# Two exp-value copies on ScalarE in the last two head pairs, and the early loads issued by SP

## The chip, the core and the metric

The program runs on one core of a Trainium2 chip. TensorE (PE) multiplies, VectorE (DVE), ScalarE (ACT) and GpSimd (POOL) work on what it leaves, and SyncE (SP) computes nothing and issues DMA transfers; ACT and POOL can issue transfers too, each on a queue of its own. The engines run side by side, each in the order of its own instructions, and wait for one another through semaphores. The metric is the device time of one execution in microseconds (us); less is better. Values are split in a high and a low part and multiplied in several passes to keep fp32 accuracy; much of the work beside PE's is copying out of the accumulation banks (PSUM) and splitting.

## The reference, cut to what matters

Causal attention with a decay bias over 2 x 8 heads, then two feed-forward layers on the 1152 tokens:

```python
scores = scale * q @ k.T + minimum(-(cum[:, None] - cum[None, :]), 0)   # causal, cum = cumsum(max(s, 0))
attn = exp(scores - max); attn = attn / (sum(attn) + 1e-9)
x = attn @ v                                    # 16 heads, S = 576, D = 64  ->  1152 x 512
x = x / sqrt(mean(x * x) + 1e-6) * rms_g
x = silu(x @ w_gate) * (x @ w_val) @ w_out      # 512 -> 1536 -> 512
h = x @ w_in                                    # 512 -> 2048
out = (h * tanh(log1p(exp(h)))) @ w_out2        # 2048 -> 512
```

## The kernel before, in words

The 16 heads are taken as 8 pairs (`NP = 8`), each in five units: units 0 to 3 are blocks of 128 query rows of one head (units 0 and 1 hold one block each's scores in one bank, 2 and 3 two banks), unit 4 is the last 64 rows of both heads. A unit goes through scores on PE (`qk_unit`), mask and row maximum on DVE (`maxes`, L468), exp on ACT (`exps`, L475), transposes of the exp values on PE (`pt_transposes`, L491), and their copies from PSUM to SBUF (`pt_evac`). For unit 3 these are two copies on DVE (L508, 128x384 and 128x512), for the other units they are on ACT (L510). After that come the products with V (`av_op`, L529, in two parts per pair), a copy to `XT` on ACT (`xt_evac`, L534), transposes back (L540) and the division by the row sums on DVE (`x_norm`, L559 and L563; the sums in `recips`, L546 to L549).

Three PSUM banks (`psT`) go round among the transposes of exp values, the transposes back and `xn_t` (L601). The last turns the normalized tokens of the first batch for the feed-forward layers while the last two pairs are computed; `xn_evac` takes it out, on ACT first (L607), and then on DVE (L608), which subtracts what ACT wrote.

Weights arrive as pieces of 512 KB (`w_load`, L315) and are unpacked by `wa` (ACT, L327), `wb` (DVE, L332 and L334) and `wc` (ACT L344, and POOL or DVE L346), one piece per pair during attention. For each pair there are loads of K and Q by POOL (L119, L122), of the cumulated sums (L125), of V (`load_v`, L140) and of the raw K and Q of the two heads (`load_raw`, L115), from which `k_lo` (L130) and `q_lo` (L136) make the low parts on POOL and DVE.

The order of every engine is written out by hand: the table `T` gives each operation a due position, counted in units (pair p begins at 5p), `at(position, function, ...)` collects all of them, and the list is run in order of the positions. An engine's instructions follow in that order, so moving a due position moves an operation in its engine's queue, and a transfer waits in the queue of the engine that issues it. In the kernel before, ACT issues `load_v` of pairs 1 to 3, `load_raw` of pairs 2 and 3, the first two weight pieces, and at the very start half of the raw of pair 0 (L151) and some constants; SP issues the rest.

Of the kernel before, what the change touches and what calls it, by code (L numbers as in the profile page):

```python
# [27 lines left out]
NP = B * H // 2  # L28
# [14 lines left out]
def tile_kernel(ctx: ExitStack, tc: tile.TileContext, kq, qq, v, s, w1, w2, rms_g, out):  # L43
    nc = tc.nc
# [449 lines left out]
    def pt_evac(i):  # L494
        p, u = divmod(i, 5)
        z, t = p % 2, t_tile.pop(i)
        if u < 2:
            cp = [(PTA[z][u], t[0][:, 0:384])]
        elif u < 4:
            cp = [(PTB[z][u - 2][:, 0:n, 128 * y:128 * y + 128], t[y][:, 0:128 * n].rearrange("p (c n) -> p c n", c=n))  # L500
                  for y, n in enumerate((3, 4))]
        else:
            cp = [(PTB[z][h][:, :, 256:320], t[0].rearrange("p (c n) -> p c n", c=4)[:, :, 64 * h:64 * h + 64])
                  for h in range(2)]
            cp += [(PTC[z][h], t[1][0:64, 64 * h:64 * h + 64]) for h in range(2)]
        for dst, src in cp:
            if u == 3:
                nc.vector.tensor_copy(out=dst, in_=src)  # L508
            else:
                nc.scalar.copy(out=dst, in_=src)  # L510
# [426 lines left out]
    def strassen(g, gaps):  # L937
# [33 lines left out]
    T = {  # L971
        "pt": (2.34, 2.02, 2.12, 2.44, 2.43), "exp": (1.65, 1.57, 0.62, 1.65, 0.84),
        "ev": (2.45, 2.48, 2.75, 2.63, 2.73), "max": (0.53, 0.2, 0.61, 0.6, 0.56), "av0": (4.48, 5.38),
        "av1": (7.66, 8.04, 8.29, 7.78, 8.36), "xte": (5.91, 9.16), "xtr": (7.48, 9.22), "rec": 6.44,
# [14 lines left out]
    def at(t, f, *args):  # L989
        events.append((t, len(events), f, args))  # L990
# [44 lines left out]
    for i in range(NU):  # L1035
        u, o = i % 5, pos[i]
        at(o, qk_unit, i)
        at(o + T["pt"][u], pt_transposes, i)
        at(o + T["exp"][u], exps, i)
        at(o + T["ev"][u], pt_evac, i)  # L1040
        at(o + T["max"][u], maxes, i)
    for p in range(NP):
        i = 5 * p
        z = "z" if p == NP - 1 else ""
        for x in range(2):
            for c, o in enumerate(T[f"av{x}{z}"]):
                at(i + o, av_op, p, x, c)
            at(i + T["xte" + z][x], xt_evac, p, x)
            at(i + T["xtr" + z][x], x_transposes, p, x)
            at(i + T["xn" + z][x], x_norm, p, x)  # L1050
        at(i + T["rec" + z], recips, p)
        if NP - NA <= p:
            n = p - NP + NA
            at(i + T["wa"], wa, n)
            if p + 1 < NP:
                at(i + T["wb"][0], wb, n, 0)
                at(i + T["wb"][1], wb, n, 1)
                at(i + T["wc"], wc, n)
        if p + 1 < NP:
            q1 = nc.scalar if p < 3 else nc.sync  # L1060
            if p:
                at(i + 0.3, load_raw, p + 1, q1)
                at(i + 0.2, load_k, p + 1)
                at(i + 0.2, load_q, p + 1)
            at(i + (T["lcum"] if p else -5.4), load_cum, p + 1)
            at(i + T["lv"], load_v, p + 1, q1)
            los, eng = (T["lo"], T["_le"]) if p else (T["lo0"], T["_l0"])
            for x in range(4):
                at(i + los[x], (k_lo, q_lo)[x % 2], p + 1, x // 2, nc.vector if eng[x] == "D" else nc.gpsimd)
    at(-7.02, load_v, 0, nc.sync)  # L1070
    at(T["lim1"], limit, 1, nc.scalar)
    at(T["lim8"], limit, 8, nc.scalar)
    for t in range(5):
        at(T["sq"][t], xn_sq, 0, t)
    for n in range(3):
# [184 lines left out]
```

## Time and profile before

| | us |
|---|---|
| median of three runs | 537.87 |
| runs | 535.26, 537.87, 539.09 |
| profiled execution | 534.09 |
| its span | 532.3 |

| engine | busy us | share of the span |
|---|---|---|
| PE | 522.0 | 98% |
| DVE | 376.3 | 71% |
| ACT | 278.4 | 52% |
| POOL | 58.7 | 11% |

The profile comes from one execution. Attention takes the first 112 us, the first feed-forward layer follows to about 336 us, and the second takes the rest. The mean granted TensorE clock is 0.986 of full speed. In the rows of a timeline the first two numbers are the start and the length in us; an engine's name with a q (ACTq, SPq) is its queue of transfers; in brackets stands how long the engine was idle before the operation and what ended that.

### The profile page before, as it was taken

To read this page: it belongs to the slowest core of one execution; us is meant where nothing else is said; L and a number is where in the kernel's file an instruction comes from. 1 tells how busy PE (TensorE), PEld (TensorE's weight loads), DVE (VectorE), ACT (ScalarE), POOL (GpSimd) and SP (SyncE) were. 2 spreads that over 40 slices of the span, in tenths; PEclk is the share of its full clock that TensorE was granted. 3 is DMA by queue.
4 is the path that set the end of the run, shared out by engine and by line. 5 is a ranking of instruction groups with operands and counts; after the bars stand their busy time and mean duration, and the time that the engine had idled before them with its cause. 6 is when DMAs were issued, how large, how long until landed. Compare 5 with 4: busy or idle time off the path is not lost.

```text
span 532.3 us, 7980 instructions
## 1 busy us (share of the span) xinstructions
PE 522.0 (98%) x2948; PEld 471.5 (89%) x2948; DVE 376.3 (71%) x787; ACT 278.4 (52%) x604; POOL 58.7 (11%) x72
## 2 busy tenths in 40 slices
PE   7999999999999999999999999999999999999997
PEld 4767777688999999999999999999889999999885
DVE  6799999954988777686578777487678667653321
ACT  5688997876353435354357655564424433333211
POOL 6245666310000000000000000000000000000000
PEclk8699999999999999999999999999999999999999
DMA  9989887212003243435155635254201000000101
GB/s 223 267 209 263 210 244 176 81 50 109 7 35 118 89 153 124 148 122 153 46 159 159 169 108 159 80 158 126 73 0 51 10 2 0 1 0 1 59 1 59
DMA packets 18782, 55.90 MB, mean 105 GB/s; under 512 B 2348, under 2 KB 2604, under 8 KB 18716
## 3 DMA queue, kind: packets, MB, share of 16 engines
q1 hardware_dynamic: 13520, 42.04, 25.6%
q0 software_dynamic: 3712, 9.70, 9.0%
q10 hardware_dynamic: 1512, 3.66, 2.3%
q8 instruction: 23, 0.38, 0.3%
q14 instruction: 15, 0.12, 0.1%
HBM read 52.73 MB, written 2.66 MB: 104 GB/s over the span
## 4 chain that ended last, share of the span: by engine, by line
PE 90%; DVE 5%; ACT 2%; DMA 2%; issue 1%; ACTq 0%; DVEq 0%
PE o L864 12%; PE gv L649 11%; PE y L794 9%; PE gv L818 8%; PE gv L667 6%; PE gv L864 6%; PE xa L529 5%; PE gv L794 5%; PE pc L691 5%; PE pd L691 5%; PE pa L691 4%; PE tp L491 4%; PE sc L443 2%; PE pb L691 2%; PE sc L444 2%; DMA r<-in_w_dram 1%
## 5 line engine op out<-in xcount | busy, mean ns | idle before, releaser
L649 PE MATMUL gv<-xh,wring 128*128 128x384 f32 x256 | 67.0, 338 | 0.2 <-DVE h_w L658 0.2
L327 ACT ACTIVATE r<-r 128x512 f32<-128x512 f32 x57 | 38.5, 679 | 31.3 <-DMA r<-in_w_dram 30.6
L334 DVE SCALAR_TENSOR_TENSOR r<-r 128x512 int32<-128x512 int32 x68 | 48.4, 712 | 3.3
L794 PE MATMUL y<-hhl,w 128*128 128x384 f32 x288 | 50.2, 334 | 0.0
L794 PEld LDWEIGHTS y<-hhl,w 128*128 128x128 f32 x288 | 49.9, 188 | 0.0
L649 PEld LDWEIGHTS gv<-xh,wring 128*128 128x128 f32 x256 | 46.4, 188 | 0.4 <-DVE h_w L658 0.3
L475 ACT ACTIVATE px<-sc,cst 128x384 f32<-128x384 f32 (+2 forms) x80 | 41.3, 530 | 6.3 <-DVE cst L468 6.3
L649 PE MATMUL gv<-xl,wring 128*128 128x384 f32 x128 | 43.0, 336 | 0.0
L667 PE MATMUL gv<-xh,wring 128*128 128x384 f32 x160 | 41.6, 336 | 0.0
L468 DVE CUSTOM_DVE_ANT_0 sc<-sc,xtm 128x384 f32<-128x384 f32 (+4 forms) x72 | 34.6, 500 | 4.8 <-PE sc L444 3.0
L491 PE MATMUL tp<-cst,px 128*128 128x128 f32 (+1 forms) x200 | 30.9, 285 | 1.9 <-DVE w L563 0.8
L685 DVE TENSOR_TENSOR glb<-u,glb 128x768 fp32r<-128x768 f32 x20 | 19.1, 955 | 15.9 <-ACT glb L684 15.7
L491 PEld LDWEIGHTS tp<-cst,px 128*128 128x128 f32 (+1 forms) x200 | 24.1, 144 | 6.7 <-issue 1.2
L529 PE MATMUL xa<-aw,px 128*64 128x320 f32 (+3 forms) x192 | 30.0, 380 | 0.0
L332 DVE TENSOR_SCALAR r<-r 128x512 int32<-128x512 int32 x68 | 29.3, 430 | 0.0
L667 PEld LDWEIGHTS gv<-xh,wring 128*128 128x128 f32 x160 | 29.0, 188 | 0.0
L864 PE MATMUL o<-wt,glb 128*128 128x512 f32 x108 | 26.9, 390 | 0.0
L667 PE MATMUL gv<-xl,wring 128*128 128x384 f32 x80 | 26.9, 336 | 0.0
L864 PE MATMUL o<-w,glb 128*128 128x512 f32 x108 | 26.5, 390 | 0.0
L346 DVE TENSOR_TENSOR w<-r,w 128x512 fp32r<-128x512 f32 x24 | 16.5, 688 | 13.8 <-ACT w L344 13.7
L776 ACT CAST hhl<-h_w 128x384 fp32r<-128x384 f32 x30 | 15.5, 516 | 19.3 <-PE y L794 12.8
L794 PE MATMUL gv<-hhl,w 128*128 128x384 f32 x144 | 25.1, 334 | 0.0
(268 smaller groups left out, 1258.0 us busy)
## 6 DMA issues: line engine op xcount, KB each, us to landing
r<-in_w_dram SPq DMA_DIRECT2D x66, 512.0 KB, 3.5
w<-in_kq_dram POOLq DMA_DIRECT2D x7, 576.0 KB, 6.2
w<-in_qq_dram POOLq DMA_DIRECT2D x7, 576.0 KB, 7.1
out_dram<-osb SPq DMA_DIRECT2D x8, 256.0 KB, 2.1
px<-in_v_dram SPq DMA_DIRECT2D x5, 320.0 KB
r<-in_w_dram ACTq DMA_DIRECT2D x2, 512.0 KB, 4.4
px<-in_v_dram ACTq DMA_DIRECT2D x3, 320.0 KB
raw_hA<-in_kq_dram SPq DMA_DIRECT2D x3, 288.0 KB
```

The lines of the kernel that those rows point to most:

```text
L327: nc.scalar.activation(out=top, in_=top, func=ACTF.Prelu, scale=2.0 ** -112, alpha=-2.0 ** 32)
L334: nc.vector.scalar_tensor_tensor(out=low, in0=top, scalar=3, in1=low, op0=ALU.logical_shift_left, op1=ALU.bitwise_or)
L468: nc.vector.tensor_tensor_reduce(out=sv, in0=sv, in1=m, scale=-0.125, scalar=first, op0=ALU.add, op1=ALU.min, accum_out=sbias[:, c:c + 1])
L475: nc.scalar.activation(out=pv, in_=sv, func=ACTF.Exp, bias=sbias[:, c + x:c + x + 1], scale=-1.0, accum_out=ssum[:, sc:sc + 1])
L491: nc.tensor.transpose(t[0:rows, o - a:o - a + 128], P[pos[i] % 2][:, o:min(e, o + 128)], ident)
L529: nc.tensor.matmul(o, V[z][0:rows, c, ds], r, start=(c == 0), stop=(c == (1, 4)[part]))
L649: nc.tensor.matmul(t[:, g, 0:TB], w[:, a, 128 * c:128 * c + 128], xhl[r][:, c, TB * b:TB * b + TB], start=(n == 0), stop=(n == 11))
L667: nc.tensor.matmul(t[:, g, 0:TB], w[:, a, 128 * c:128 * c + 128], xhl[r][:, c, TB * b:TB * b + TB], start=(n == 0), stop=(n == 11))
L691: nc.tensor.matmul(t, A[a][:, 128 * c:128 * c + 128], B[r][:, c], start=(start and n == 0), stop=(n == 5), skip_group_check=True)
L794: nc.tensor.matmul(y_t[b][d], w[:, a, 128 * d:128 * d + 128], hhl[:, r], start=(f == FY[0] and y == 0), stop=(f == FY[-1] and y == 2))
L818: nc.tensor.matmul(t[:, x, 0:TB], w[:, a, 128 * c:128 * c + 128], xhl[r][:, c, TB * b:TB * b + TB], start=(n == 0), stop=(n == 11))
L864: nc.tensor.matmul(o_t[b][tt], gl[:, r, x, 128 * tt:128 * tt + 128], w[:, a], start=(g == 0 and x == 0 and y == 0), stop=(g == NG - 1 and ...
```

## The change

In the last two pairs (p = 6 and 7) the two copies of unit 3 go to ACT. The weight operation `wa` of pair 7 is due 0.64 positions later and `wc` of pair 6's due list 0.35 later; in ACT's order that puts both behind `xn_evac` of the fourth quarter (due 40.73), `wc` first (40.80), then `wa` (40.85). All nine loads that ACT issued inside the loop over pairs are issued by SP (L151 and the constants stay), in their old order but for the second weight piece, which is due just behind `load_v` instead of just ahead of it.

```diff
         for dst, src in cp:
-            if u == 3:
+            if u == 3 and p < NP - 2:
                 nc.vector.tensor_copy(out=dst, in_=src)
             else:
                 nc.scalar.copy(out=dst, in_=src)
...
-        "lcum": 1.47, "lv": 3.58, "lim1": 2.19, "lim8": 8.49, "sq": (24.04, 23.82, 29.07, 27.0, 28.42),
+        "lcum": 1.47, "lv": 3.58, "lim1": 2.19, "sq": (24.04, 23.82, 29.07, 27.0, 28.42),
...
             n = p - NP + NA
-            at(i + T["wa"], wa, n)
+            at(i + T["wa"] + (0.64 if p == NP - 1 else 0), wa, n)
             if p + 1 < NP:
                 at(i + T["wb"][0], wb, n, 0)
                 at(i + T["wb"][1], wb, n, 1)
-                at(i + T["wc"], wc, n)
+                at(i + T["wc"] + (0.35 if p == NP - 2 else 0), wc, n)
         if p + 1 < NP:
-            q1 = nc.scalar if p < 3 else nc.sync
             if p:
-                at(i + 0.3, load_raw, p + 1, q1)
+                at(i + 0.3, load_raw, p + 1)
                 at(i + 0.2, load_k, p + 1)
                 at(i + 0.2, load_q, p + 1)
             at(i + (T["lcum"] if p else -5.4), load_cum, p + 1)
-            at(i + T["lv"], load_v, p + 1, q1)
+            at(i + T["lv"], load_v, p + 1)
...
-    at(T["lim1"], limit, 1, nc.scalar)
-    at(T["lim8"], limit, 8, nc.scalar)
+    at(T["lim1"], limit, 1)
+    at(T["lv"] + 5.01, limit, 8)
```

## Rows read from the trace of the kernel before

**Rows 1.** The page, busy tenths in 40 slices of the span, PE
```profile
PE   7999999999999999999999999999999999999997
```

**Rows 2.** Table of stages: length, then PE, PEld, DVE, ACT, POOL busy, clock, DMA
```profile
22.00:23.00 1.00, 1.00 (x5) 0.92 (x4) 0.00 (x0) 1.00 (x6) 0.01 (x1) 0.54 1.29 332
...
91.20:102.30 11.10, 9.73 (x69) 6.78 (x69) 10.63 (x33) 8.40 (x28) 5.20 (x7) 1.00 0.30 97
102.30:112.00 9.70, 8.96 (x68) 6.37 (x68) 7.07 (x21) 8.01 (x23) 1.54 (x2) 1.00 0.01 2
```

**Rows 3.** Timeline of PE, last two pairs
```profile
95.84 0.72 PE L491 MATMUL tp<-cst,px 128*128 128x128 f32 x5
...
108.96 0.30 PE L491 MATMUL tp<-cst,px 128*64 128x128 f32 x1 [0.47 <-DVE xl L608]
109.19 2.45 PE L529 MATMUL xa<-aw,px 128*64 128x320 f32 x20
```

**Rows 4.** Timeline of ACT, last two pairs
```profile
94.57 1.13 ACT L607 ACTIVATE xh<-bank,cst 128x512 fp32r<-128x512 f32 x2
...
104.42 0.98 ACT L510 COPY aw<-tp 128x384 f32<-128x384 f32 x2
...
106.30 0.68 ACT L327 ACTIVATE r<-r 128x512 f32<-128x512 f32 x1
...
107.43 0.89 ACT L607 ACTIVATE xh<-bank,cst 128x512 fp32r<-128x512 f32 x2
...
108.52 1.09 ACT L510 COPY aw<-tp 128x256 f32<-128x256 f32 x4
```

**Rows 5.** Timeline of DVE, last two pairs
```profile
94.40 1.15 DVE L508 COPY aw<-tp 128x384 f32<-128x384 f32 x2
95.47 0.94 DVE L608 SCALAR_TENSOR_TENSOR xl<-bank,cst,xh 128x512 fp32r<-128x512 f32 x2
...
108.15 0.94 DVE L608 SCALAR_TENSOR_TENSOR xl<-bank,cst,xh 128x512 fp32r<-128x512 f32 x2 [0.44 <-ACT xh L607]
```

**Rows 6.** Timeline of ACT and its queue, first two pairs
```profile
17.30 0.36 ACTq L140 DMA_DIRECT2D px<-in_v_dram  x1
17.50 0.37 ACT L475 ACTIVATE px<-sc,cst 128x128 f32<-128x128 f32 x1
...
29.25 0.33 ACTq L315 DMA_DIRECT2D r<-in_w_dram  x1
30.74 0.34 ACTq L140 DMA_DIRECT2D px<-in_v_dram  x1
31.12 0.43 ACT L534 COPY xtm<-xa 128x320 f32<-128x320 f32 x1 [1.40 <-PE xa L529]
...
34.41 0.45 ACTq L115 DMA_DIRECT2D raw_r<-in_kq_dram  x1
...
34.94 0.66 ACT L327 ACTIVATE r<-r 128x512 f32<-128x512 f32 x1
```

**Rows 7.** Timeline of DVE, pairs 1 and 2
```profile
28.84 1.89 DVE L334 SCALAR_TENSOR_TENSOR r<-r 128x512 int32<-128x512 int32 x1
...
40.70 0.69 DVE L334 SCALAR_TENSOR_TENSOR r<-r 128x512 int32<-128x512 int32 x1
```

**Rows 8.** Timeline of POOL, pairs 1 and 2
```profile
28.77 1.41 POOL L136 TENSOR_TENSOR w<-raw_hA,w 64x576 fp32r<-64x576 f32 x1 [6.76 <-DMA raw_hA<-in_kq_dram]
...
40.99 1.66 POOL L136 TENSOR_TENSOR w<-raw_mm,w 64x576 fp32r<-64x576 f32 x1 [2.89 <-DMA raw_mm<-in_kq_dram]
```

**Rows 9.** Timeline of PE, pairs 0 and 1
```profile
18.47 0.61 PE L450 MATMUL sc<-w 68*128 68x288 f32 x1 [0.42 <-ACT px L475]
...
35.51 0.74 PE L491 MATMUL tp<-cst,px 128*128 128x128 f32 x5 [0.84 <-DVE w L563]
```

**Rows 10.** View of one line, L315, the weight loads: time from issue to landing
```profile
DMA to landing us min/median/max: 3.4/3.6/5.3
```

**Rows 11.** DMA queues from 35 to 39 us: packets, MB, share
```profile
q10 hardware_dynamic: 8, 0.02, 1.5%
```

## The prediction

> **What bounds the kernel now.** I read the page's slices first: TensorE is 9 tenths busy or more in every slice but the first and the last [rows 1]. Time can be won or lost only where it stands still or where its clock is low, and what is lost ahead of such a stretch reaches the end unshortened. Then the stages: the edits touch two. Late, in the last two pairs, TensorE is busy 9.73 of 11.10 us and 8.96 of 9.70 us; the standing of 1.37 + 0.74 = 2.11 us is all that the late edits could ever win. [...]
>
> Then I read the timelines of the engines in the last two pairs. TensorE's rows show five transposes at 95.84 (unit 4 of pair 6) and, at 108.96, the last transpose of pair 7, held for VectorE's L608, directly ahead of the last 20 attention products at 109.19 [rows 3]. ScalarE is the fuller engine from 104.42 on: its rows follow one another without a hole up to the four copies at 108.52 [rows 4]. VectorE does the copies in question of pair 6 at 94.40 and then L608 at once [rows 5].
>
> **The late edits, step by step.** VectorE loses four copies, two in each pair; those of pair 6 take 1.15 us [rows 5]. ScalarE gains them. Their price there is seen in the same two shapes of unit 2: the two that begin at 104.42 take 0.98 us [rows 4]. What lies behind them in ScalarE's order decides.
>
> Pair 6: the copies come ahead of `xn_evac` (L607), which first starts at 94.57 [rows 4]. With 0.98 us before it that becomes about 95.5. VectorE's L608 needs L607's first half. In pair 7 L607 starts at 107.43 [rows 4] and L608, held by it, at 108.15 [rows 5], 0.72 us later. So L608 starts at 95.5 + 0.6 to 0.7 = 96.1 or 96.2, where it starts at 95.47 now [rows 5]: VectorE is given 1.15 us and waits them away. The fifth transpose of the row at 95.84 [rows 3] writes the bank that this L608 empties (three banks go round in the order in which the code asks for them). It comes about 0.5 us later, and with it all that TensorE has behind it. I take **+0.5**. Bounds: 0, if the bank is free earlier than I read; +0.98, the full copies.
>
> Pair 7: the two offsets put `wa` and `wc`, which run from 106.30 to 107.43 now, behind `xn_evac` [rows 4]. That clears 1.13 us for 0.98 us of copies, so L607 and L608 keep their places, and so does the transpose at 108.96. But `wa` and `wc` still stand ahead of the copies at 108.52 [rows 4], and those come 0.98 us later. The products at 109.19 [rows 3] read what they write. Four copies take 1.09 us [rows 4], so the two that the first products need end near 109.06; 0.13 us is spare and some 0.8 us shows. I take **+0.8**. Bounds: 0, if ScalarE gets there earlier; +0.98. VectorE's relief in pair 7 buys nothing: TensorE waits for it only through L608, which L607 times.
>
> Late edits together: 0.5 + 0.8 = **+1.3 us**, bounds 0 and +1.96.
>
> **The early edits, step by step.** ScalarE loses nine DMA issues. The one at 17.30 lasts 0.36 us, yet the exp behind it already starts at 17.50, so it is hidden; the one at 30.74 holds its successor 0.38 us, to 31.12, after 1.40 us in which ScalarE waited for the products anyway [rows 6]. VectorE is the late engine in that pair (below), so I count 0.
>
> SP issues in the order of the code. So the weight load of 29.25 stands behind load_v, which waits for the products until 30.74; it is issued at about 31.12, with 320 KB ahead of it. It must land before L327 at 34.94, which stands in ScalarE's order ahead of the exps [rows 6]. Loads of this kind land after 3.4 to 5.3 us [rows 10]: at 34.5 to 36.4, a stall of 0 to 1.5 us. I take 0, since the median of 3.6 gives 34.7. The upper end is what a tail caught by POOL's loads would bring: from 35 to 39 us the queue of ScalarE's loads moved 0.02 MB [rows 11], though raw loads had been issued on it up to 34.41 [rows 6].
>
> [...]
>
> The raw loads of pair 2 come forward, because SP does not stand behind exps. Today POOL's `q_lo` waits 6.76 us for them and starts at 28.77 [rows 8]. VectorE's L334, which starts at 28.84, then takes 1.89 us, where the same operation takes 0.69 a pair later [rows 7], and TensorE stands 0.84 us at 35.51 for VectorE [rows 9]. With raw early, POOL starts earlier, when its other input has landed. Bounds: -0.84, the whole stand won, if POOL is through before VectorE comes; +0.84, if two POOL operations block VectorE where one does now. I take **+0.3**: POOL then meets L332 as well as L334.
>
> **Sum.** 1.3 + 0.3 = +1.6 us. The profiled execution took 534.09 us (a span of 532.3 and 1.8 around it), which gives 535.7. It was faster than all the runs shown, 3.8 us under their median of 537.87, so against the median I predict **539.5 us**, 0.3% more.
>
> **Rivals.**
>
> [...] From pair 2 on the order is kept by a hair: VectorE's L334 starts at 40.70 [rows 7], POOL's `q_lo` at 40.99 [rows 8], 0.29 us later. POOL's start follows transfers, and a delay of TensorE moves those only a pair later. If pair 1 loses more than 0.29 us, or raw lands that much earlier, POOL is first, L334 waits, and the next pair starts late in turn. Price: 0.84 us of standing [rows 9] in each of five pairs, 4.2 us: 539.5 + 4.2 = 543.7 us, with a stalled L327 up to 545. Against it: pair 1 collides today and pair 2 recovers.
> [...]
>
> *B, the late cost is hidden.* ScalarE or the banks have more room than I read, both late steps cost nothing, and the move to SP only changes a queue: 537.87 + 0.3 = 538.2 us, no change.
>
> [...]
>
> **How the numbers follow.** Forecast 0.50, A 0.20, B 0.17, C 0.13. About 1% (5.4 us) is what a measurement of this kernel can tell from no change; the runs of before lie between 535.26 and 539.09. Slower by over 1%, above 543.2, takes A in full: 0.15. Faster by over 1%, under 532.5, needs C, the stand at 35.51 and a free late part at once: 0.04. Within 1%: 0.81. The range: below, C's 537.1 less 1.6 us for the spread of the runs, 535.5; above, A's 543.7, so 544. The forecast's own range is 537.5 to 541.5.
>
> **What would show it.** Late: L608 of pair 6 held by L607 with VectorE idle before it; the fifth transpose of unit 4 waiting for L608; the four copies of pair 7 starting after `wa`, and the 20 products behind them 1.3 us later, counted from the first products of pair 6. It is wrong if those 20 products come as early as now. Early: POOL's `q_lo` of pair 2 before 28.77, L332 or L334 long beside it, and TensorE standing at about 35.5 for 0.8 to 1.7 us. [...] If the total comes out right with none of these, the reasons were wrong.

## The result and the profile after

| kernel | runs | median us | lowest to highest | profiled execution | its span |
|---|---|---|---|---|---|
| before | 13 | 536.36 | 533.37 to 540.56 | 534.09 | 532.3 |
| after | 13 | 539.01 | 537.01 to 542.36 | 542.36 | 540.4 |

After takes 1.0061 of the time of before, 95% interval 1.0038 to 1.0084: 0.6% slower. The interval leaves out 1, so a difference under the 1% that the prediction took as its bound can be told from none. In this document a run over 1.5% above the quickest of its kernel counts as slow and is left out of ratios and medians, which takes one run from best_sp (544.60 us) and four from the runs of before beside fence, fence_after and both_late. The two profiled executions lie 8.27 us apart and the medians 2.65: the profile of after is the slowest of its thirteen runs, that of before a quick one. So I take positions inside a stage from the profiles, not their difference in total.

A simple measure of the late part is the distance from the seven transposes of unit 3 in pair 6 (L491) to the first gate product (L649), with those of pair 7 between them. First before, then after:

```profile
92.12 0.98 PE L491 MATMUL tp<-cst,px 128*128 128x128 f32 x7
...
105.97 0.98 PE L491 MATMUL tp<-cst,px 128*128 128x128 f32 x7
...
107.86 0.63 PE L491 MATMUL tp<-cst,px 128*128 128x128 f32 x4 [0.26 <-DVE aw L508]
...
111.76 0.42 PE L649 MATMUL gv<-xh,wring 128*128 128x384 f32 x1
```

```profile
99.44 0.98 PE L491 MATMUL tp<-cst,px 128*128 128x128 f32 x7
...
113.54 0.98 PE L491 MATMUL tp<-cst,px 128*128 128x128 f32 x7
...
120.45 0.42 PE L649 MATMUL gv<-xh,wring 128*128 128x384 f32 x1
```

In before it runs from 92.12 to 111.76 us, 19.64 us; in after from 99.44 to 120.45, 21.01 us. Up to pair 6, after is 7.32 us behind; in the late part it loses 1.37 more. Of the 7.32 us, 5.9 are there by 64 us, behind the two early stands shown below and a fallen clock after each (0.50 from 25 to 27 us and from 49 to 55). The rest comes behind 86 us, where TensorE stands 0.97 us for L608 at 96.92, in unit 2 of pair 6; late_only, with the loads of before, has the same stand (0.98 us), so it isn't put to the loads.

TensorE in the slices of the page of after (before: [rows 1]), and its granted clock under them:

```profile
PE   6898999889999999999999999999999999999997
...
PEclk9797999999999999999999999999999999999999
```

What is lost lies in the first nine slices, as in the prediction; the rest of the row is unchanged. The clock is down (7 tenths) in the second and the fourth slice and not in the last pairs.

The late part of after on TensorE, ScalarE and VectorE (start and length in us; answers to [rows 3 to 5]):

```profile
100.86 0.63 PE L601 MATMUL bank<-cst,w 128*128 128x128 f32 x4 [0.44 <-DVE w L563]
...
103.84 0.30 PE L491 MATMUL tp<-cst,px 128*64 128x128 f32 x1 [0.42 <-DVE xl L608]
...
116.58 0.30 PE L491 MATMUL tp<-cst,px 128*64 128x128 f32 x1 [0.72 <-DVE xl L608]
117.63 2.69 PE L529 MATMUL xa<-aw,px 128*64 128x320 f32 x20 [0.76 <-ACT aw L510]
```

```profile
101.44 0.97 ACT L510 COPY aw<-tp 128x384 f32<-128x384 f32 x2
102.28 0.92 ACT L607 ACTIVATE xh<-bank,cst 128x512 fp32r<-128x512 f32 x2
...
114.14 1.00 ACT L510 COPY aw<-tp 128x384 f32<-128x384 f32 x2
115.04 0.90 ACT L607 ACTIVATE xh<-bank,cst 128x512 fp32r<-128x512 f32 x2
115.82 0.66 ACT L344 CAST wring<-r 128x512 fp32r<-128x512 f32 x1
116.36 0.68 ACT L327 ACTIVATE r<-r 128x512 f32<-128x512 f32 x1
116.93 0.37 ACT L534 COPY xtm<-xa 128x256 f32<-128x256 f32 x1
117.18 0.85 ACT L510 COPY aw<-tp 128x256 f32<-128x256 f32 x4
```

```profile
103.03 0.94 DVE L608 SCALAR_TENSOR_TENSOR xl<-bank,cst,xh 128x512 fp32r<-128x512 f32 x2 [1.53 <-ACT xh L607]
...
115.77 0.94 DVE L608 SCALAR_TENSOR_TENSOR xl<-bank,cst,xh 128x512 fp32r<-128x512 f32 x2 [1.88 <-ACT xh L607]
```

In pair 6, ScalarE does its two copies and only then L607; VectorE, which has been given their time, stands 1.53 us for L607, and TensorE's fifth transpose 0.42 us for L608. In pair 7, L344 and L327 stand between L607 and the four copies, and the 20 products wait 0.76 us for those.

The early part of after, on DMA queues and engines, in order of the fences: SP's and GpSimd's issues, TensorE, VectorE, ScalarE.

```profile
15.13 0.33 SPq L315 DMA_DIRECT2D r<-in_w_dram  x1
15.51 0.43 SPq L140 DMA_DIRECT2D px<-in_v_dram  x1
15.98 0.43 SPq L115 DMA_DIRECT2D raw_hA<-in_kq_dram  x1
16.52 0.36 SPq L115 DMA_DIRECT2D raw_hB<-in_kq_dram  x1
```

```profile
16.25 0.56 POOL L125 DMA_DIRECT2D w<-scr  x1 [4.38 <-DMA cst<-in_rms_g_dram]
```

```profile
22.59 0.30 PE L444 MATMUL sc<-w 68*128 68x128 f32 x1 [1.41 <-DMA w<-scr]
...
48.34 0.45 PE L443 MATMUL sc<-w 128*128 128x128 f32 x1 [1.80 <-POOL w L130]
```

```profile
28.80 1.13 DVE L332 TENSOR_SCALAR r<-r 128x512 int32<-128x512 int32 x1
...
30.03 1.72 DVE L334 SCALAR_TENSOR_TENSOR r<-r 128x512 int32<-128x512 int32 x1
```

```profile
36.41 0.68 ACT L327 ACTIVATE r<-r 128x512 f32<-128x512 f32 x1 [0.34 <-DMA r<-in_w_dram]
```

The raw loads of pair 2 are issued before 17 us, where ScalarE issued them at 21.84 and 22.27. GpSimd is early in pair 1 and collides with L332 and L334, as forecast: its `q_lo` runs from 28.23 us for 1.40 and its `k_lo` from 29.71 for 1.49, and L332 takes 1.13 us beside the first and L334 1.72 beside the second, where the shortest of each in after take 0.42 and 0.69. But TensorE stands in two places that the prediction doesn't name, 1.41 us for the cumulated sums (`w<-scr`) and 1.80 us for `k_lo`. The second stand has a late transfer behind it too: GpSimd's load of Q for pair 3, issued at 34.75, takes 10.1 us to land, and `q_lo`, with `k_lo` behind it, starts at 44.98. In before the same load, issued at 33.17, takes 7.0 us, and `q_lo` starts at 40.99 [rows 8].

The table of stages of after, microsecond by microsecond (length, then PE, PEld, DVE, ACT, POOL busy, granted clock, DMA, GB/s; before: [rows 2]):

```profile
17.00:18.00 1.00, 0.99 (x5) 0.76 (x4) 0.97 (x3) 0.79 (x4) 1.00 (x1) 0.66 0.90 359
...
21.00:22.00 1.00, 0.18 (x1) 0.04 (x1) 0.60 (x3) 0.64 (x3) 0.56 (x2) 1.00 1.04 198
22.00:23.00 1.00, 0.41 (x3) 0.41 (x3) 0.00 (x0) 1.00 (x5) 0.00 (x0) 1.00 1.38 175
...
25.00:26.00 1.00, 1.00 (x7) 0.96 (x5) 0.72 (x4) 0.23 (x2) 0.00 (x0) 0.50 1.41 240
```

The clock leaves 0.50 in the microsecond from 17 and is at 1.00 before the stand, where before still has 0.54 at 22. Behind the stand it is at 0.50 again by 25 us. Both executions begin unit 3 of pair 0 at 23.47 us: the early rise is given back. The fall then costs 1.6 us more: the eight products (L529) that begin at 26.77 us in before begin at 28.35 in after.

### The profile page after: what moved, and what is told of

It reads as the page before. It is cut to its first block, busy times and chain, and to the rows that moved or that the text cites. A ratio compares the mean times of both kernels' runs of the same rounds, so it can differ in the third digit from the quotient of the medians.

```text
span 540.4 us, 7976 instructions
## 1 busy us (share of the span) xinstructions
PE 524.1 (97%) x2948; PEld 473.6 (88%) x2948; DVE 379.7 (70%) x783; ACT 280.6 (52%) x608; POOL 57.5 (11%) x72
## 4 chain that ended last, share of the span: by engine, by line
PE 87%; DVE 5%; ACT 3%; DMA 2%; issue 2%; SPq 1%; DVEq 0%; ACTq 0%
PE o L864 12%; PE gv L649 12%; PE y L794 9%; PE gv L818 8%; PE gv L667 8%; PE gv L864 6%; PE pa L691 5%; PE pc L691 5%; PE pd L691 5%; PE gv L794 5%; PE xa L529 4%; PE tp L491 3%; PE pb L691 2%; PE sc L443 2%; DVE sc L468 2%
## 5 line engine op out<-in xcount | busy, mean ns | idle before, releaser
L649 PE MATMUL gv<-xh,wring 128*128 128x384 f32 x256 | 67.1, 338 | 0.2 <-DVE h_w L658 0.2
L327 ACT ACTIVATE r<-r 128x512 f32<-128x512 f32 x57 | 38.4, 677 | 29.2 <-DMA r<-in_w_dram 29.0
L334 DVE SCALAR_TENSOR_TENSOR r<-r 128x512 int32<-128x512 int32 x68 | 50.3, 739 | 3.4
L649 PEld LDWEIGHTS gv<-xh,wring 128*128 128x128 f32 x256 | 46.4, 188 | 0.4 <-DVE h_w L658 0.3
L649 PE MATMUL gv<-xl,wring 128*128 128x384 f32 x128 | 43.0, 336 | 0.0
L491 PE MATMUL tp<-cst,px 128*128 128x128 f32 (+1 forms) x200 | 33.2, 298 | 2.8 <-DVE xl L608 2.1
L491 PEld LDWEIGHTS tp<-cst,px 128*128 128x128 f32 (+1 forms) x200 | 25.8, 152 | 8.4 <-DVE xl L608 2.8
L529 PE MATMUL xa<-aw,px 128*64 128x320 f32 (+3 forms) x192 | 30.1, 379 | 0.8 <-ACT aw L510 0.8
L332 DVE TENSOR_SCALAR r<-r 128x512 int32<-128x512 int32 x68 | 30.5, 448 | 0.0
L685 DVE TENSOR_TENSOR glb<-u,glb 128x768 fp32r<-128x768 f32 x20 | 19.1, 955 | 15.9 <-ACT glb L684 15.7
L443 PE MATMUL sc<-w 128*128 128x384 f32 (+1 forms) x64 | 25.5, 408 | 2.5 <-POOL w L130 1.8
```

What stands on the lines that cost most here:

```text
L327: nc.scalar.activation(out=top, in_=top, func=ACTF.Prelu, scale=2.0 ** -112, alpha=-2.0 ** 32)
L334: nc.vector.scalar_tensor_tensor(out=low, in0=top, scalar=3, in1=low, op0=ALU.logical_shift_left, op1=ALU.bitwise_or)
L491: nc.tensor.transpose(t[0:rows, o - a:o - a + 128], P[pos[i] % 2][:, o:min(e, o + 128)], ident)
L529: nc.tensor.matmul(o, V[z][0:rows, c, ds], r, start=(c == 0), stop=(c == (1, 4)[part]))
L649: nc.tensor.matmul(t[:, g, 0:TB], w[:, a, 128 * c:128 * c + 128], xhl[r][:, c, TB * b:TB * b + TB], start=(n == 0), stop=(n == 11))
```

## The experiments

All runs in one table. Pair 6 is the distance from unit 3's transposes in pair 6 to those in pair 7, pair 7 the one from there to the first gate product, both in the profiled execution. Ratios are to runs of the kernel before on the same chip; a single run has none.

| kernel | median us (runs) | ratio, 95% interval | pair 6 | pair 7 |
|---|---|---|---|---|
| before (profile) | 536.36 (13) | | 13.85 | 5.79 |
| after | 539.01 (13) | 1.0061 [1.0038, 1.0084] | 14.10 | 6.91 |
| late_only | 538.88 (12) | 1.0064 [1.0029, 1.0099] | 14.11 | 6.91 |
| loads_only | 537.52 (12) | 1.0023 [0.9994, 1.0052] | 13.85 | 5.79 |
| pair6_only | 537.82 (1) | | 15.67 | 5.79 |
| pair7_only | 536.63 (1) | | 13.49 | 6.92 |
| fence | 536.36 (12) | 0.9988 [0.9954, 1.0022] | 15.89 | 5.79 |
| fence_after | 539.86 (12) | 1.0095 [1.0066, 1.0125] | 15.90 | 8.53 |
| both_late | 535.50 (12) | 0.9986 [0.9953, 1.0018] | 13.87 | 5.81 |
| norm_first | 535.15 (12) | 0.9970 [0.9939, 1.0002] | 13.44 | 5.78 |
| best | 534.15 (12) | 0.9948 [0.9919, 0.9976] | 13.56 | 5.82 |
| best_sp | 536.82 (11) | 1.0005 [0.9974, 1.0037] | 13.93 | 5.81 |
| best_raw | 535.19 (12) | 0.9983 [0.9953, 1.0013] | 13.55 | 5.81 |
| best_noraw | 535.82 (12) | 1.0001 [0.9969, 1.0033] | 13.55 | 5.81 |

**The change in parts.** The late edits alone and the loads alone; then each pair's late edits alone.

```diff
-            if u == 3:
+            if u == 3 and p != NP - 2:      # pair6_only; pair7_only: p != NP - 1, with the two offsets of wa and wc
```

> The late edits alone (four copies on ScalarE, the two offsets), loads issued as before. Theory 1, both parts cost: about 1.4 us over before (ratio 1.002 to 1.003), and from the row of seven transposes of pair 6 to the first gate product 21.0 us, as in the changed kernel, against 19.64 before. Theory 2, the early loads cost everything and the longer last pairs follow from them: ratio 1.000 and 19.6 us. Theory 3, the late edits cost everything: ratio 1.005 to 1.006.

> All nine loads issued by SP, the late edits left out. Theory 1: about 1.3 us over before (ratio 1.002 to 1.003), the last pairs at 19.6 us, and the loss ahead of them, where TensorE waits for operands of K and Q that land late. Theory 2: ratio 1.005 to 1.006. Theory 3: ratio 1.000.

> Only the two copies of pair 6 on ScalarE, no offset. By the steps of the prediction TensorE loses 0.3 to 0.5 us between the seven transposes of pair 6 and those of pair 7 (13.85 us before, 14.10 in the changed kernel), because VectorE's L608 waits for L607. Rival: the loss there comes with the early loads, and this interval stays at 13.85.

> Only the two copies of pair 7 on ScalarE, with the two offsets. By the steps of the prediction the 20 products start 0.8 us later after the seven transposes of pair 7, and the first gate product comes 0.8 to 1.1 us later (5.79 us before, 6.91 in the changed kernel), since wa and wc stand ahead of the last copies. Rival: ScalarE catches up and it stays at 5.8.

The late edits give the late part of after to 0.01 us: 14.11 + 6.91 = 21.02. The loads alone leave it as it was, 19.64. In time the late edits are slower clear of noise, 3.4 us (0.0064 x 535.79), interval 1.6 to 5.3, which is nearer to theory 3 than to theory 1. The loads alone measure 1.2 us, interval -0.3 to 2.8, which fits both. On top of the late edits they show no cost: after, with both, has 1.0061, late_only 1.0064. TensorE does wait for operands of K and Q in loads_only, as theory 1 has it: 0.57 us for `k_lo` at 45.63, behind a load of Q that takes 9.4 us.

Pair 6 of pair7_only has the code of before and takes 13.49, not 13.85. TensorE's stands in pair 6, first the kernel before, then pair7_only:

```profile
93.90 0.63 PE L601 MATMUL bank<-cst,w 128*128 128x128 f32 x4 [0.80 <-DVE w L563]
```

```profile
95.53 0.63 PE L601 MATMUL bank<-cst,w 128*128 128x128 f32 x4 [0.44 <-DVE w L563]
```

The execution of before stood 0.36 us longer for L563, which is the whole 13.85 - 13.49. After and late_only stand 0.44 and 0.43 us there. So against its like the edit of pair 6 costs 14.10 - 13.49 = 0.61 us, and that of pair 7 6.91 - 5.79 = 1.12 us: 1.73 us together. Counted from unit 3's transposes, L608 of pair 6 starts 0.60 us later in after (3.59) than in pair7_only (2.99).

pair6_only was the surprise, 15.67 us for a pair that takes 14.11 in late_only. Tables of stages, three equal stretches from the start of unit 3's transposes, pair6_only and then late_only (which has the same code in this pair):

```profile
94.30:97.30 3.00, 2.00 (x16) 1.47 (x14) 2.03 (x7) 3.00 (x9) 0.79 (x1) 1.00 0.01 3
97.30:100.30 3.00, 2.57 (x13) 2.14 (x14) 2.31 (x8) 2.57 (x11) 3.00 (x5) 0.75 0.49 124
100.30:103.30 3.00, 3.00 (x16) 1.87 (x15) 2.87 (x10) 2.02 (x8) 0.22 (x1) 0.68 0.74 231
```

```profile
100.20:103.20 3.00, 1.99 (x17) 1.44 (x14) 2.07 (x7) 2.99 (x9) 0.75 (x1) 1.00 0.01 3
103.20:106.20 3.00, 2.58 (x18) 2.10 (x18) 2.28 (x8) 2.65 (x13) 3.00 (x5) 1.00 0.44 98
106.20:109.20 3.00, 3.00 (x21) 1.87 (x21) 2.87 (x10) 2.78 (x10) 0.26 (x1) 1.00 0.65 255
```

TensorE is busy to within 0.01 us alike, and in one execution the clock falls behind the stands and in the other it does not. That is 15.67 - 14.11 = 1.56 us.

**Is it GpSimd's collisions that make executions differ?** In the kernel fence GpSimd reads one element that L334 has written before it goes on, so that it never runs ahead of L332 and L334; fence_after is the changed kernel with the same.

```diff
-        "lo": (3.28, 3.14, 4.19, 4.89),
+        "lo": (3.48, 3.47, 4.19, 4.89),
...
+    def behind_wb(n):
+        nc.gpsimd.tensor_copy(out=fence_t, in_=conv[n][0:1, 0:1, 0])
...
+            if p:
+                at(i + 3.465, behind_wb, p - 1 - NP + NA)
```

> The kernel before, and in pairs 1 to 6 GpSimd reads one element of what VectorE's L334 wrote before it starts q_lo and k_lo of the next pair (their due positions go from 3.14 and 3.28 to 3.47 and 3.48), so that GpSimd is never ahead of L332 and L334. Theory 1, rival A of the prediction is what makes one execution differ from the next: wherever GpSimd is first, L332 or L334 takes 1.1 to 1.9 us, TensorE stands for VectorE, and the same code reaches pair 6 at 92.1 us in one execution and at 100.3 us in another. Then L332 and L334 take no more than 0.5 and 0.8 us in all pairs up to 105 us, pair 6's transposes of unit 3 start at 91 to 92.5 us, the median falls by 1 to 2.5 us against the kernel before (ratio 0.995 to 0.998) and the runs lie closer together, within 4 us. Theory 2, the executions differ by the time at which transfers land: the ratio is 1.000 within 0.002 and the runs lie over 6 us as before.

> The changed kernel with the same order between L334 and GpSimd. Theory 1: from unit 3 of pair 6 to the first gate product it takes 21.0 us (before 19.6), and its median lies above that of the fenced kernel before by the late edits alone, 1.2 to 1.6 us. Rival, the loads on SP cost something beside collisions (raw, V and weights of SP beside K, Q and the cumulated sums of GpSimd): above it by 2.5 us or more, with TensorE held for w<-scr near 22 us or for k_lo and q_lo that start late because K or Q landed late.

The view of L334 up to 105 us in fence (its shortest, median and longest duration in ns):

```profile
L334 DVE SCALAR_TENSOR_TENSOR r<-r x7: 693/695/699, 29.2 to 103.5; 128x512 int32<-128x512 int32 x7
```

The collisions are gone, and the runs still lie from 534.13 to 539.78 us with a ratio of 0.9988; pair 6's transposes of unit 3 start at 94.04 us, not at 91 to 92.5. Theory 1 falls: an L334 of 1.7 us or more is seen in before (1.89), after (1.72), pair6_only (1.71) and both_late (1.70), but collisions are not what makes executions differ. The ratio is the one that theory 2 gives, but nothing here tests its cause. What the rows show of a collision is its length: 1.89 us for the L334 that starts 0.07 us behind GpSimd's `q_lo` [rows 7, 8], against 0.70 at most here. What in the chip holds L334 they do not show.

fence_after lies 3.5 us above fence (539.86 - 536.36), and the signs of its rival are there: TensorE stands 1.69 us for `w<-scr` at 22.73 and 0.70 us for `k_lo` at 47.77. But late_only alone measured 3.4 us, so this difference can't be put to the loads.

The last pair of fence_after shows a fallen clock once more. TensorE's timeline there:

```profile
114.03 0.30 PE L491 MATMUL tp<-cst,px 128*64 128x128 f32 x1 [0.72 <-DVE xl L608]
115.08 4.33 PE L529 MATMUL xa<-aw,px 128*64 128x320 f32 x20 [0.75 <-ACT aw L510]
```

The two stands are those of after, but the 20 products take 4.33 us, not 2.69, under a lower clock (0.50 in the microseconds from 116 to 119; in after 1.00 throughout): pair 7 takes 8.53 us, 1.62 more, and the late part 24.4 us, not the 21.0 of theory 1. In pair 6, fence and fence_after take 15.9 us, with a fallen clock (0.50 from 98.04 to 101.04 us in fence, from 99.10 to 102.10 in fence_after) after two stands, of 1.25 or 1.26 and of 0.57 or 0.58 us.

**The order on ScalarE.** The copies stay on ScalarE in both pairs, and all weight work is put behind the copies of unit 4.

```diff
-            if u == 3:
+            if u == 3 and p < NP - 2:
...
-            at(i + T["wa"], wa, n)
+            at(i + T["wa"] + (1.64 if p >= NP - 2 else 0), wa, n)
...
-                at(i + T["wc"], wc, n)
+                at(i + T["wc"] + (1.35 if p >= NP - 3 else 0), wc, n)
```

> The kernel before; the two copies of unit 3 are on ScalarE in the last two pairs as in the change, but wa and wc are put behind the four copies of unit 4 in both pairs (wa 1.64, wc 1.35 positions later), not ahead of them. All loads as before. Theory, the steps of the prediction: what costs time is what stands ahead of L607 in pair 6 and ahead of the four copies in pair 7. With 1.2 us of weight work out of both places for 0.98 us of copies, pair 6 takes 13.5 to 13.9 us from unit 3's transposes to those of pair 7 (before 13.85, changed 14.10) and pair 7 takes 5.5 to 5.9 us from there to the first gate product (before 5.79, changed 6.91). Rival, ScalarE has simply too much work in the last two pairs and the order changes only where it shows: the sum from pair 6 to the gate product stays above 20.5 us. The time is that of the kernel before, ratio 0.998 to 1.002, by the theory, and 1.002 to 1.006 by the rival.

The last pair of both_late, ScalarE and then TensorE:

```profile
110.22 1.02 ACT L510 COPY aw<-tp 128x384 f32<-128x384 f32 x2 [0.16 <-PE tp L491]
111.14 0.90 ACT L607 ACTIVATE xh<-bank,cst 128x512 fp32r<-128x512 f32 x2
111.91 0.38 ACT L534 COPY xtm<-xa 128x256 f32<-128x256 f32 x1
112.17 0.68 ACT L510 COPY aw<-tp 128x256 f32<-128x256 f32 x2
```

```profile
112.67 0.30 PE L491 MATMUL tp<-cst,px 128*64 128x128 f32 x1 [0.72 <-DVE xl L608]
112.90 2.42 PE L529 MATMUL xa<-aw,px 128*64 128x320 f32 x20
```

The copies follow L607 with only L534 between them, and the products have no stand of their own. Pair 7 is back to 5.81 us, the sum to 19.68, with the same work on ScalarE. So in pair 7 the order costs the time, not the load, and the rival falls there. In pair 6 the order wins back part: 13.87 us, where the edit as made takes 14.10 and pair7_only, with the copies on VectorE, 13.49. The time, 0.9986 of before, can't be told from 1, and its interval (up to 1.0018) lies below that of late_only (from 1.0029): the order shows in the time too.

**A version that is faster.** norm_first puts VectorE's `q_lo` behind the division; best is both_late with that, and with the copies of pair 7 shared between VectorE and ScalarE.

```diff
-        "lo": (3.28, 3.14, 4.19, 4.89),
+        "lo": (3.28, 3.14, 4.19, 5.495),
...
+            if u == 3 and (p < NP - 2 or p == NP - 1 and y == 0):    # best: copy y = 0 of pair 7 stays on VectorE
```

> The kernel before, with VectorE's q_lo (L136) of every pair placed behind the division L559 and L563 instead of just ahead of it (due 5.495 instead of 4.89). In the looks so far TensorE stood for L563 once or twice in most executions: 0.84 us in the kernel before at 35.5 us, 1.79 with the late edits alone, 2.20 with the weight work behind, and 0.80 to 1.26 us ahead of L601 in pair 6. L136 takes 0.75 us. Theory 1, these stands are what VectorE's lateness costs, and the clock that falls behind one in some executions (from 1.00 to 0.50 for some 3.3 us, 1.6 to 2.0 us lost) is why executions differ: then the stands for L563 shrink by up to 0.75 us each, pair 6 takes 13.0 to 13.5 us instead of 13.85, and the median falls by 0.5 to 2 us (ratio 0.996 to 0.999). Theory 2, VectorE has the same work and is late one operation further on: the stands move behind L136 (TensorE waits for the scores of the next pair's second unit) and the ratio is 1.000 within 0.002.

> The weight work behind the unit-4 copies in both last pairs, L136 behind L563, and in pair 7 one of the two copies of unit 3 on VectorE and one on ScalarE; loads as before. Theory 1: L607 of pair 7 starts some 0.5 us earlier than with both copies on ScalarE, so pair 7 takes 5.2 to 5.5 us (before 5.79) and pair 6 13.2 to 13.6 us (before 13.85); median 1 to 2.5 us below the kernel before, ratio 0.995 to 0.998. Theory 2: pair 7 as in the run with both copies on ScalarE, 5.8 us, and no difference in the time.

In norm_first the stands for L563 are gone and pair 6 takes 13.44 us, within the 13.0 to 13.5 expected; its ratio, 0.9970, is as expected, but the interval still holds 1, and the runs spread over 6.9 us, as before, so that these stands make executions differ is not shown. And part of the stand moved on to the bank behind it, which TensorE now awaits for 1.15 instead of 0.57 us:

```profile
95.91 0.24 PE L601 MATMUL bank<-cst,w 64*128 64x64 f32 x1 [1.15 <-DVE aw L508]
```

best is faster than the kernel before, 2.8 us by its ratio (0.0052 x 537.01), interval 1.3 to 4.4, and its runs lie from 533.19 to 536.96. Which of its edits brings the time is not shown: the intervals of both_late, norm_first and best overlap, and in the profile of best TensorE still stands for L563 early, 0.72 us at 33.92 and 1.15 us at 46.61. Sharing the copies brought nothing, a miss: ScalarE's one copy waits for its transposes, and L607 of pair 7 starts 1.51 us after unit 3's transposes (108.96 - 107.45), where both_late has 1.50.

```profile
108.47 0.59 ACT L510 COPY aw<-tp 128x512 f32<-128x512 f32 x1 [0.59 <-PE tp L491]
108.96 0.90 ACT L607 ACTIVATE xh<-bank,cst 128x512 fp32r<-128x512 f32 x2
```

**Which loads.** best_sp issues all nine by SP, best_raw the four raw loads of pairs 2 and 3, best_noraw the other five (the change's edits of `load_v` and of the two `limit` lines).

```diff
-                at(i + 0.3, load_raw, p + 1, q1)
+                at(i + 0.3, load_raw, p + 1)      # best_raw
```

> The same kernel with all nine loads issued by SP, as in the change. Theory 1, the loads on SP cost 1 to 1.5 us in the middle of the runs (1.3 measured alone, 2.1 between the two fenced kernels less the 1.4 of the late edits): ratio to the same kernel with ScalarE's loads 1.002 to 1.003, TensorE held for w<-scr near 22 us in an execution in which the clock rises before 21 us, and K and Q landing later. Rival, the move of the loads costs nothing and the difference seen so far is what executions differ by: within 0.5 us of the same kernel with the loads on ScalarE.

> The best kernel so far, with the four raw loads of pairs 2 and 3 on SP and V and the weights left on ScalarE. Theory, the raw loads are what costs: SP issues those of pair 2 at 15.4 to 16.5 us, ScalarE does so at 21.8 and 22.3 us, and their 576 KB go ahead of the small w<-scr of GpSimd that the first scores of pair 1 need. Then TensorE is held 1 to 1.7 us for w<-scr near 22 to 24 us, as in three of the four looks with SP's loads, and the time is 1.5 to 3 us above the same kernel with ScalarE's loads (ratio to the kernel before 0.998 to 1.001, as in the run with all nine on SP). Rival, V and the weights cost it, or all nine together: no stand for w<-scr and a ratio as for the best kernel, 0.993 to 0.996.

> The best kernel so far, with V and the first two weight pieces on SP (five of the nine loads) and the raw loads left on ScalarE. Theory: no stand for w<-scr, and the time of the kernel with ScalarE's loads (ratio to the kernel before 0.993 to 0.996). Rival: the stand for w<-scr is there as well, or L327 waits for its weight piece near 35 us, and the ratio is 0.998 to 1.001.

TensorE waits for `w<-scr` in best_sp (1.66 us) and in best_raw (the row below), and not in best or best_noraw:

```profile
22.52 0.30 PE L444 MATMUL sc<-w 68*128 68x128 f32 x1 [1.46 <-DMA w<-scr]
```

Over all profiles this stand is there in four of the five with SP's raw loads and in none of the nine in which ScalarE issues them. The transfer itself is longer in all five: `w<-scr` lands 6.0 to 8.0 us after its issue, in the nine others after 3.5 to 4.7 us. In loads_only, the fifth, it takes 6.0 us too, but the clock rose late (0.54 in the microsecond from 21) and TensorE came to the product only at 22.14 us, just behind the landing. So the raw loads bring the late landing, and with an early TensorE the stand. In all four profiles with the stand the clock falls behind it: its mean from 23 to 30 us is 0.76 in each. In none of the other ten does it fall there; the mean is 1.00.

With all nine loads on SP a second transfer is longer: K and Q of pair 3, which GpSimd issues between 31 and 36 us, take 8.2 to 9.2 and 8.8 to 10.1 us (after, loads_only, fence_after, best_sp), in the ten other profiles 5.2 to 6.9 and 5.8 to 8.3. In those four TensorE then stands for `k_lo` between 45 and 49 us (1.80, 0.57, 0.70 and 0.15 us), elsewhere only in fence (0.55 us).

The time follows only in part. best_sp is 2.7 us above best (536.82 - 534.15, timed side by side), more than the 1 to 1.5 us of theory 1; its rival, within 0.5 us, falls. But best_raw and best_noraw, timed on another chip without best beside them, both have ratios above that of best. best_raw has the stand and a ratio (0.9983) as its theory says; best_noraw has no stand, as its theory says, but 1.0001 for the 0.993 to 0.996 expected, and the three intervals overlap. That the nine loads together cost time in best is measured once, with ratio intervals that just touch (up to 0.9976, from 0.9974); which of them does stays open.

## Why the prediction was right, and where its steps were not

The total was forecast at 539.5 us and came out at 539.01; the sign and the late mechanism were right. That the total came so near is luck in part, two errors that cancel. The base was the median of three runs, 537.87 us; that of thirteen is 536.36, 1.5 us lower. The difference was forecast at 1.6 us and is 2.65 in the medians, 3.3 by the ratio (interval 2.0 to 4.5): the sum was too small.

1. *Pair 6, +0.5 us.* Against its like it cost 0.61 us, by the path that was named: L607 late, L608 late by 0.60 us (0.6 to 0.7 forecast), the fifth transpose late. The plain difference of the two first profiles, 0.25, hides this behind another stand that was 0.36 us shorter.
2. *Pair 7, +0.8 us.* It cost 1.12. L607, L608 and the last transpose kept their places, counted from unit 3's transposes in pair 7 (from 105.97 us in before and 113.54 in after): the last transpose came after 3.04 us (before 2.99). The copies came 1.09 us later (3.64 instead of 2.55) and the products began 0.87 later (4.09 instead of 3.22), where 0.8 was forecast. The term was short by the rest: the group of products itself took 2.69 instead of 2.45 us. That TensorE waits for VectorE only through L608 was misread: the row at 107.86 of before shows 0.26 us for VectorE's copy itself. That stand went, the one for L608 grew from 0.47 to 0.72, and nothing was won, as forecast.
3. *Early, +0.3 us.* The loads alone measured +1.2 (-0.3 to 2.8), so the size isn't refuted, but the steps were partly wrong. The collision came, L332 and L334 both long (1.13 and 1.72 us); the stand at 35.5 us for VectorE did not come with it; TensorE reached pair 1's transposes of unit 2 at 33.38 us by then, 1.57 later than in before (31.81), which may be why. L327 stalled 0.34 us, inside 0 to 1.5. The step that failed is the one that looked only at what reads the raw data. It did not ask what else was under way when those 576 KB moved some 6 us forward: the 37 KB of `w<-scr`, issued at 16.25, held TensorE until 22.59, and GpSimd's K and Q loads near 34 us took 3 us longer to land (9.2 and 10.1 us, before 6.2 and 7.0).
4. *What the sum left out: the clock.* The stands of the late part account for 1.73 us, and the forecast puts the loss by a clock that falls again at nothing. The mean granted clock over the runs is 0.9892 for before (23 runs beside late_only and loads_only), 0.9871 for late_only, and 0.9862 for loads_only and for after. An estimate from these, the difference from before times 536 us, gives 1.1 us for late_only and 1.6 us for the other two. With the 1.73 us of stands that makes 2.8 us for late_only and 3.3 us for after, where 3.4 and 3.3 were measured; for loads_only it makes 1.6 us, where 1.2 was measured. So the missing part has the size of the added time at the lower clock. It stays an estimate: it takes TensorE as bound by its clock throughout, the clocks of the runs of before beside after are not on record (the other sets of before have 0.9892 to 0.9898), and within the runs of one kernel time follows the clock only weakly (last section). So this term is likely, not shown.
5. *Rival A, collisions that repeat.* They do repeat: L334 takes 1.7 us or more in three pairs of after (0.69 in the others) and in four of pair6_only (1.71 at 88.26), whose loads are those of before. But the price was wrong: without any of them the time is 0.9988 of before, a gain of at most 2.5 us by the interval where 4.2 was put.
6. *Rival C, an earlier clock.* Its 537.1 us, from which the range is worked out, takes 2.45 us off; no run shows that term. The clock did rise earlier in after, some 5 us: the microsecond from 17 has 0.66, as that from 22 has 0.54 in before. It did so as well in best (0.64 in the microsecond from 17), pair6_only (a mean of 0.64 from 14 to 18 us) and both_late (0.98 from 18 to 23), whose loads ScalarE issues, and by only about 1 us in loads_only (0.54 in the microsecond from 21). The rival's condition was that TensorE's stand for the exp goes; it was still there (0.57 us at 18.56, before 0.42 [rows 9]). So that condition was wrong. The gain is real, in place of the 2.45 us it is 1.7 us where no stand follows (unit 3 of pair 0 begins at 21.78 us in best, 23.47 in before), and in after it was spent on the next stand. Rival B, a hidden late cost, falls with the 1.73 us.

The 37 KB of `w<-scr` land 6.2 us after their issue in after, and still after 4.7 us in best, where the raw loads come later. What held them no row shows.

## What to carry to other kernels

When work is moved to another engine, count what then stands ahead of each producer in that engine's order, and move the work that nobody waits for behind the producers: here the same copies cost 1.7 us (21.02 against 13.49 + 5.79) or 0.4 us (19.68 against the same), depending only on where the weight operations `wa` and `wc` stood. When a load is moved forward, look at the small transfers that are under way at its new time, not only at its own readers: here 37 KB landed after 6.0 to 8.0 us instead of 3.5 to 4.7. Compare like with like before a difference of two traces is called a cost: one stand that an edit doesn't touch can differ by 0.4 us from execution to execution, and a fallen clock by 1.6. And look at the forecast difference, not only at the total: here a base 1.5 us too high hid a sum that was too small.

## What was not expected of the hardware

TensorE's granted clock fell from 1.00 to 0.50 behind short stands in some executions and not in others with the same stands: 1.56 us in pair 6 (pair6_only against late_only) and 1.62 us in pair 7 (fence_after against after). The stands ahead of these falls are 0.43 to 0.75 us long; in pair 6 of the fenced kernels, where it falls too, up to 1.26. What decides whether it falls no run shows. Executions of one code differ by 7 us (before: 533.37 to 540.56), and a fallen clock is one cause that the traces show. It explains only a part: over the four sets of runs of before in the experiments, a lower mean granted clock goes with a longer time only weakly (correlations of -0.30, -0.37, -0.46 and 0.21).
